# Summing the row partial sums of w_down by 32x32 VectorE transposes and selector matmuls, and merging two small copies at the start, in a decode kernel (conditioned layer norm, cached grouped attention, gated FFN)

## The chip, the cores and the metric

The kernel runs on one core of a Trainium2 chip. The metric is device time in microseconds (us) of one execution, as the median over several executions.

"The profile" below is the summary page of one profiled execution, with its views: groups, waits, chain of waits, timeline and windows. "The trace" is the record of every instruction and every DMA packet behind it. PE is TensorE's matmuls, PEld its weight loads, DVE VectorE, ACT ScalarE, POOL GpSimd, and SPq the SyncE queue that issues the loads.

## The reference, cut to what matters

```python
x = A_x                                        # 1 x 1 x 1024, bfloat16
mod = (_silu(c) @ w_mod).reshape(...)          # six modulation vectors of 1024
h = _layernorm(x) * (1 + ca) + sa
x = x + ga * attention(h, k_cache, v_cache, wq, wo)   # 32 heads, 4 kv heads, 65536 cached positions
h = _layernorm(x) * (1 + cb) + sb
x = x + gb * ((_gelu(h @ w_gate) * (h @ w_up)) @ w_down)  # F = 3584
```

Every weight and both caches are read once. There is one token, so the kernel moves 185.6 MB and computes little per byte.

## The kernel before

Loads are issued by SyncE into a ring of ten slots that are one tensor in SBUF, `slots`. SBUF tensors are placed one after the other in the order in which they are allocated.

```python
    ident = sb("ident", [P, P], dt.bfloat16)   # 256 bytes in each partition
    x_col = sb("x_col", [P, KD])               # 32 bytes
    x_nat = sb("x_nat", [P, KD])
    sg_col = sb("sg_col", [P, KD])
    th_col = sb("th_col", [P, KD])
    slot_all = nc.alloc_sbuf_tensor("slots", [P, NSLOT * SLOT], dt.bfloat16)
    identf = sb("identf", [P, P])
    ...
    c_col = sb("c_col", [P, KD])
```

The last product, with w_down, is done in two ways. Most of w_down ("early") is used as the moving operand, 512 columns at a time, against 32-column weights that hold the activations; the sums are rows, at partitions 0, 32, 64 and 96 of two PSUM banks. The part that lands last ("late": pieces of 1024, 512, 256 and 256 KB) is used as weights, 128x128 at a time, against one activation column, and accumulates columns in `acc_dn`. The rows must be added into those columns:

```python
        v = row_matvec(place_d, early, o_pad, (v_uc,), (NQ - 1, NROW * UE - NQ))
        v_rows = both(row_a, 2, P)             # PSUM -> SBUF: one half on VectorE, one on ScalarE
        late = j_d[len(early):]
        col_matvec(acc_dn, late[:1], o_pad[:, :, 0], KD, True)
        PE.wait(*v_rows)
        for j, a in enumerate(plain):          # 8 blocks of 128 columns, fp32
            pe.matmul(
                acc_dn[:, j:j + 1], row_a[:, a], ones1[:, :], start=False, stop=True, skip_group_check=True)
        v = col_matvec(acc_dn, late[1:], o_pad[:, :, 0], KD, False)
        # then: multiply by gb, add x1, one transpose, copy, store
```

Of the kernel before, what the change touches and what calls it, by code (L numbers as in the profile page):

```python
# [5 lines left out]
ACT = mybir.ActivationFunctionType  # L6
ALU = mybir.AluOpType
AX = mybir.AxisListType

P = 128  # L10
# [12 lines left out]
ROW = 512  # L23
QD = 32
# [56 lines left out]
def bass_adaLN_cond__gqa_block_cached__geglu_ffn__decode_kernel(  # L81
# [15 lines left out]
    KD = D // P  # L97
# [14 lines left out]
    scale = float(DH) ** -0.5  # L112
    NQ = P // QD
# [5 lines left out]
    PE = Eng(nc, nc.tensor, "c_pe")  # L119
    DVE = Eng(nc, nc.vector, "c_dve")  # L120
    AC = Eng(nc, nc.scalar, "c_act")
    GP = Eng(nc, nc.gpsimd, "c_pool")
    sp, pe, dve, act, pool = nc.sync, nc.tensor, nc.vector, nc.scalar, nc.gpsimd
# [4 lines left out]
    def sb(name, shape, d=dt.float32):  # L128
        return nc.alloc_sbuf_tensor(name, shape, d)

    ident = sb("ident", [P, P], dt.bfloat16)
    x_col = sb("x_col", [P, KD])
    x_nat = sb("x_nat", [P, KD])
    sg_col = sb("sg_col", [P, KD])
    th_col = sb("th_col", [P, KD])
    slot_all = nc.alloc_sbuf_tensor("slots", [P, NSLOT * SLOT], dt.bfloat16)
    identf = sb("identf", [P, P])
    ones1 = sb("ones1", [P, 1])
    onesf = ones1[:, :].to_broadcast([P, P])
    halfneg = sb("halfneg", [P, 1])  # L140
    c_col = sb("c_col", [P, KD])
    s_pad = sb("s_pad", [P, KD, QD], dt.bfloat16)
    h_pad = sb("h_pad", [P, KD, QD], dt.bfloat16)
    ga_nat = sb("ga_nat", [P, KD])
# [5 lines left out]
    x1_col = sb("x1_col", [P, KD])  # L150
# [10 lines left out]
    NR = P // REP  # L161
    m_sp = sb("m_sp", [P, 2, NR])
    rsel = sb("rsel", [P, NR])
    selt = sb("selt", [P, P])
    s_fp = s_pad[:, :, :].rearrange("p k c -> p (k c)").bitcast(dt.float32)
    mneg, al, zr = (s_fp[:, i * NC:(i + 1) * NC] for i in range(3))
# [8 lines left out]
    def ktf(half):  # L175
        return kt_sb[:, half, :, :].rearrange("p a b -> p (a b)").bitcast(dt.float32)
# [5 lines left out]
    row_a = ktf(1)[:, 0:2 * ROW]  # L182
# [10 lines left out]
    b6 = nc.alloc_psum_tensor("b6", [P, 512], dt.float32)  # L193
    b7 = nc.alloc_psum_tensor("b7", [P, 512], dt.float32)
    kt_fp = kt_ps[:, :].bitcast(dt.float32)
    tr_ps = sc_ps[:, 0:2 * ROW]
    acc_dn = b7[:, 64:64 + KD]
# [53 lines left out]
    def emit_all():  # L251
# [39 lines left out]
        for i in range(0, NC + KU, KU):  # L291
# [6 lines left out]
            if i >= KU:  # L298
                j = i - KU
# [53 lines left out]
        for a in [a for r in ev for a in r] + ex + m1 + oc + pc + kfill + vfill:  # L353
# [5 lines left out]
            selw[:, HQ - REP:HQ].unsqueeze(2), identf[:, :].rearrange("p (r h) -> p h r", h=REP), AX.X, ALU.add)  # L359
        dve.tensor_reduce(  # L360
            rsel[:, :].unsqueeze(2), identf[:, :].rearrange("p (r h) -> p r h", h=REP), AX.X, ALU.add)
        v = DVE.done(dve.tensor_reduce(
            dm4.unsqueeze(3), identf[:, :].rearrange("p (c b h) -> p c b h", c=NQ, h=REP), AX.X, ALU.add))
        DVE.wait(v)
# [3 lines left out]
        v_sel = DVE.done(dve.tensor_reduce(  # L368
            dmask[:, :].unsqueeze(2), dm4.rearrange("p c b -> p b c"), AX.X, ALU.add))
# [4 lines left out]
        PE.wait((x_sem, 16))  # L374
        v = PE.done(pe.matmul(b6[:, 2 * KD:3 * KD], x_row, ident[0:KD, 0:KD], start=True, stop=True))
        DVE.wait(v)
        cx = b6[:, 0:2 * KD].rearrange("p (k c) -> p c k", c=2)
        v_c = DVE.done(dve.tensor_copy(c_col[:, :], cx[:, 0, :]))
        AC.wait(v_c)
        v_th = AC.done(act.activation(th_col[:, :], c_col[:, :], ACT.Tanh, scale=0.5))  # L380
        dve.tensor_copy(x_col[:, :], cx[:, 1, :])
        v_x = DVE.done(dve.tensor_copy(x_nat[:, :], b6[:, 2 * KD:3 * KD]))
        DVE.wait(v_th)
        v = DVE.done(dve.tensor_scalar(sg_col[:, :], th_col[:, :], 0.5, 0.5, ALU.mult, ALU.add))
        DVE.wait(v)
        v_s = DVE.done(dve.tensor_tensor(s_pad[:, :, 0], c_col[:, :], sg_col[:, :], ALU.mult))

        def col_matvec(bank, jobs, rhs, nblk, first):

# [49 lines left out]
        def ln_norm(xin, ready, pscol):  # L439

            st = once("st", [P, 2])
            junk = once("junk", [P, KD])
            me = once("me", [P, 2])
            sq = once("sq", [P, 1])
            va = once("va", [P, 1])
            rs = once("rs", [P, 1])
            hn = once("hn", [P, KD])
            DVE.wait(ready)
            dve.reduce_sum(st[:, 0:1], xin, axis=AX.X)
            v = DVE.done(dve.tensor_tensor_reduce(junk[:, :], xin, xin, 1.0, 0.0, ALU.mult, ALU.add, st[:, 1:2]))  # L450
            PE.wait(v, t1)
            v = PE.done(pe.matmul(b6[:, pscol:pscol + 2], onesf, st[:, :], start=True, stop=True))
            DVE.wait(v)
            v = DVE.done(dve.tensor_scalar(me[:, :], b6[:, pscol:pscol + 2], 1.0 / D, None, ALU.mult))
            DVE.wait(v)
            v = DVE.done(dve.tensor_tensor(sq[:, :], me[:, 0:1], me[:, 0:1], ALU.mult))
            DVE.wait(v)
            v = DVE.done(
                dve.scalar_tensor_tensor(va[:, :], me[:, 1:2], LN_EPS, sq[:, :], ALU.add, ALU.subtract)  # L459
            )  # L460
            GP.wait(v, v_const)
            v = GP.done(pool.tensor_tensor(rs[:, :], va[:, :], halfneg[:, :], ALU.pow))  # L462
            DVE.wait(v)
            v = DVE.done(dve.tensor_scalar(hn[:, :], xin, me[:, 0:1], rs[:, 0:1], ALU.subtract, ALU.mult))
            return hn, v
# [18 lines left out]
        plain = [slice(j * P, (j + 1) * P) for j in range(KD)]  # L484
# [1 line left out]
        def quads(t, n, w=P):  # L486
            return t.rearrange("p (n g y) -> p n g y", n=n, g=w // QD)[:, :, :, 0]

        hn1, v_hn1 = ln_norm(x_col[:, :], v_x, 32)

        def place_m(k):
            for h in range(2):
# [38 lines left out]
        def place_2(b0, n):  # L531
# [5 lines left out]
        v = row_matvec(place_2(0, 2 * NQ), whole(j_q), h_pad, (v_h,), (0, KD - 1), rest_of_mod)  # L537
# [4 lines left out]
        v = turn(tr_ps, P, row_q, plain, P, (v_ra, v_rb))  # L542
        DVE.wait(v)
        v = DVE.done(dve.tensor_copy(
            q_col[:, :].rearrange("p (r g t) -> p r t g", r=2, g=NQ),
            quads(tr_ps, KD).rearrange("p (r t) g -> p r t g", r=2)))
# [146 lines left out]
        v_x = {}  # L693
# [96 lines left out]
        for g in range(Hkv):  # L790
            ins = pe.matmul(
                b6[0:HQ, 0:P + ZW], selw[:, HQ - REP * (g + 1):HQ - REP * (g + 1) + QD], o_red[:, g, :],
                start=g == 0, stop=g == Hkv - 1)
        v = PE.done(ins)
        DVE.wait(v)
        v = DVE.done(dve.reciprocal(rz[:, :], b6[0:HQ, P + ZW - 1:P + ZW]))
        DVE.wait(v)
        v = DVE.done(dve.tensor_scalar(oT[:, :], b6[0:HQ, 0:P], rz[:, 0:1], None, ALU.mult))
        PE.wait(v, v_const)
        w = P // QW  # L800
        for q in range(QW):
            ins = pe.matmul(
                b6[:, 352:352 + w], spread[:, QW - 1 - q:QW - 1 - q + P], oT[:, q * w:(q + 1) * w],
                start=q == 0, stop=q == QW - 1)
        v = PE.done(ins)
# [7 lines left out]
        def both(rows, b0, n):  # L813
            DVE.wait(v)
            x = DVE.done(dve.tensor_copy(rows[:, 0:ROW], kt_fp[:, b0 * ROW:(b0 + 1) * ROW]))  # L815
            AC.wait(v)
            y = AC.done(act.activation(  # L817
                rows[0:n, ROW:2 * ROW], kt_fp[0:n, (b0 + 1) * ROW:(b0 + 2) * ROW], ACT.Copy))
            return x, y

        last_ev = tuple(ev[(NC - 1) % SITES][b].tok(seen_by(NC - 1)) for b in range(NB))
        v = row_matvec(place_o, whole(j_o), o_pad, (v_opk,) + last_ev, (NQ - 1, HQ - NQ))
        t_att = sb("t_att", [P, KD])
        v_rows = both(row_a, 0, P)
        v = turn(tr_ps, P, row_a, mixed, P, v_rows)
# [2 lines left out]
        DVE.wait(v_ac)  # L828
        v = DVE.done(dve.tensor_tensor(t_att[:, :], t_att[:, :], mod_sb[:, 2, :], ALU.mult))
        DVE.wait(v)  # L830
        v_x1 = DVE.done(dve.tensor_tensor(x1_col[:, :], t_att[:, :], x_col[:, :], ALU.add))
        hn2, v = ln_norm(x1_col[:, :], v_x1, 34)
        v_tn = turn(tr_ps, P, row_a, plain, P, (v_ac,))
        v_h2 = modulate(h_pad, hn2, v, 3, 4)
# [1 line left out]
        v = DVE.done(dve.tensor_reduce(att_nat[:, :].unsqueeze(2), quads(tr_ps, KD), AX.X, ALU.add))  # L836
        DVE.wait(v)
        v_tf = v
        v = DVE.done(dve.tensor_tensor(att_nat[:, :], att_nat[:, :], ga_nat[:, :], ALU.mult))
# [19 lines left out]
        v = row_matvec(place_2(2, NBF), whole(j_g), h_pad, (v_h2,), (0, KD - 1))  # L859
        v_rows = both(row_g, 2, QD * (NBF - NQ))  # L860
        v_g = turn_f(row_g, v_rows + (v_tf,))
        DVE.wait(v_g)
        for dst, src in zip(parts(g1), parts_ps()):
            v = DVE.done(dve.tensor_copy(dst, src))
        v_g1 = v
        DVE.wait(v)
        v = DVE.done(dve.tensor_tensor(g2, g1, g1, ALU.mult))
        DVE.wait(v)
        v = DVE.done(dve.tensor_scalar(g3, g2, GELU_C, 1.0, ALU.mult, ALU.add))
        DVE.wait(v)  # L870
        v = DVE.done(dve.tensor_tensor(g4, g3, g1, ALU.mult))
        AC.wait(v)
        v = AC.done(act.activation(gth, g4, ACT.Tanh, scale=SQRT_2_OVER_PI))
        DVE.wait(v)
        v = DVE.done(dve.scalar_tensor_tensor(g2, gth, 1.0, g1, ALU.add, ALU.mult))
        v_g2 = v
        v = row_matvec(place_2(0, NBF), whole(j_u), h_pad, (v_h2,), (0, KD - 1))
        v_rows = both(row_u, 0, QD * (NBF - NQ))
# [7 lines left out]

        early = [a for a in j_d if a[2] < NROW * UE]
        v = row_matvec(place_d, early, o_pad, (v_uc,), (NQ - 1, NROW * UE - NQ))
        v_rows = both(row_a, 2, P)
        late = j_d[len(early):]  # L890
        col_matvec(acc_dn, late[:1], o_pad[:, :, 0], KD, True)
        PE.wait(*v_rows)
        for j, a in enumerate(plain):
            pe.matmul(  # L894
                acc_dn[:, j:j + 1], row_a[:, a], ones1[:, :], start=False, stop=True, skip_group_check=True)
        v = col_matvec(acc_dn, late[1:], o_pad[:, :, 0], KD, False)
        DVE.wait(v, v_xn)
        v = DVE.done(dve.tensor_tensor(t_dn, acc_dn, gb_nat[:, :], ALU.mult))
        DVE.wait(v)
        v = DVE.done(dve.tensor_tensor(y_col, t_dn, x1_nat[:, :], ALU.add))  # L900
        PE.wait(v)
        yT = b6[:, :].bitcast(dt.bfloat16)[0:KD, 768:768 + P]
        v = PE.done(pe.transpose(yT, y_col, ident[:, :]))
        DVE.wait(v)
        v = DVE.done(dve.tensor_copy(y_row, yT))
# [3 lines left out]
        assert issued[0] == len(loads)  # L909

    emit_all()
    return nc

# [27 lines left out]
```

## Time and profile before

| | before |
|---|---|
| median time | 439.82 us (3 runs, 438.96 to 439.94) |
| span of the profiled execution | 438.6 us |
| read from HBM | 185.60 MB, 423 GB/s over the span |
| last loads of w_down land at | 430.96, 432.21, 432.84, 433.49 us |

The landing times are the last of a load's 16 semaphore updates in the trace.

From the page of the kernel before: DMA is the busy share of the 16 DMA engines in 40 slices of the span, in tenths.

```profile
PE   0436559959696878959777895968779594675376
DMA  8999999999999999999999999999999999999994
GB/s 355 430 435 439 435 432 429 429 424 433 433 430 433 431 433 430 433 436 430 436 439 433 436 428 430 430 439 430 436 430 430 430 426 429 444 428 434 415 430 173
```

The DMA engines are full from the second slice to the last but one, so the kernel's time is the time of the loads plus what is left to do after the last of them.

The end of the timeline of the kernel before (start, duration of the merged group, engine, line, operation, out<-in, shapes, count, and the idle time before it with what ended it):

```profile
429.68 0.60 ACT L817 ACTIVATE kt_sb<-kt_ps 128x512 f32<-128x512 f32 x1 [9.14 <-PE kt_ps L419]
429.68 0.69 DVE L815 COPY kt_sb<-kt_ps 128x512 f32<-128x512 f32 x1 [6.82 <-PE kt_ps L419]
431.01 1.01 PE L396 MATMUL b<-p_row,slots 128*128 128x1 bf16 x32 [1.40 <-DMA slots<-in_B_w_down_dram]
431.89 3.55 PE L894 MATMUL b<-ones,kt_sb 128*128 128x1 f32 x16
435.30 0.99 PE L396 MATMUL b<-p_row,slots 128*128 128x1 bf16 x32
436.33 0.17 DVE L898 TENSOR_TENSOR kt_sb<-b,gb_nat 128x8 f32<-128x8 f32 x1 [5.96 <-PE b L396]
437.30 0.37 SPq L907 DMA_DIRECT2D out_dram<-kt_sb  x1
```

Line 894 is the eight fp32 matmuls that add the rows; each appears as two records. They occupy TensorE from 431.89 to 435.30 us, and the last 32 column matmuls (line 396) start behind them although their data had landed by 433.49 us. The chain of waits, which goes back from the last instruction to whatever released each step, runs through the block (start, duration, engine, tile, line, count; it counts the block from the end of the group ahead of it):

```profile
431.01 1.01 PE b L396 x32
432.02 3.41 PE b L894 x16
435.44 0.87 PE b L396 x32
```

### The profile page before, as it was taken

What the parts mean: (1) busy time and instruction counts of PE and PEld (TensorE: products, weight loads), DVE (VectorE), ACT (ScalarE), POOL (GpSimd) and SP (SyncE); (2) the same over time, 40 slices, a digit from 0 to 9 for tenths busy, and PEclk for the clock granted to TensorE, in tenths of its full rate; (3) what the DMA queues carried; (4) which work ended last, traced back from release to release, by engine and by line L of the source; (5) the groups of instructions that cost most, each with busy time, mean ns of one, the idle gap of its engine ahead of it and who ended that gap; (6) DMA issues with size and microseconds to landing.
All of it is one profiled execution on the core that took longest, in us unless ns stands there. A gap on an engine that the chain in (4) does not pass through costs nothing.

```text
span 438.6 us, 8499 instructions
## 1 busy us (share of the span) xinstructions
PE 305.5 (70%) x3892; PEld 203.4 (46%) x3892; DVE 206.9 (47%) x309; ACT 111.8 (25%) x165; POOL 16.8 (4%) x23
## 2 busy tenths in 40 slices
PE   0436559959696878959777895968779594675376
PEld 0112236636464556646555563646556362232124
DVE  6601025637383765827465673737477373421001
ACT  1000001533332523333351443324135334000000
POOL 9500000000000000000000000000000000000000
PEclk9995669999696988979897896969689798587665
DMA  8999999999999999999999999999999999999994
GB/s 355 430 435 439 435 432 429 429 424 433 433 430 433 431 433 430 433 436 430 436 439 433 436 428 430 430 439 430 436 430 430 430 426 429 444 428 434 415 430 173
DMA packets 7936, 185.77 MB, mean 424 GB/s; under 512 B 882, under 2 KB 882, under 8 KB 1268
## 3 DMA queue, kind: packets, MB, share of 16 engines
q1 hardware_dynamic: 7904, 185.60, 98.4%
q8 instruction: 8, 0.13, 0.1%
q14 instruction: 4, 0.03, 0.0%
q10 hardware_dynamic: 20, 0.01, 0.0%
HBM read 185.60 MB, written 0.00 MB: 423 GB/s over the span
## 4 chain that ended last, share of the span: by engine, by line
DMA 56%; PE 31%; DVE 10%; issue 1%; ACT 1%; POOL 0%; POOLq 0%; SPq 0%
DMA slots<-in_A_k_cache_dram 44%; PE kt_ps L597 16%; DMA slots<-in_B_w_down_dram 8%; PE b L667 4%; DMA slots<-in_A_v_cache_dram 4%; PE sc_ps L619 4%; PE kt_ps L419 3%; DVE selt L365 3%; DVE kt_sb L705 2%; DVE s_pad L739 1%; DVE o_red L728 1%; PE b L894 1%; PE sc_ps L648 1%; PE b L635 1%; DVE o_acc L716 1%
## 5 line engine op out<-in xcount | busy, mean ns | idle before, releaser
L597 PE MATMUL kt_ps<-ident,slots 128*128 128x128 bf16 x2048 | 156.8, 238 | 48.6 <-DMA slots<-in_A_k_cache_dram 47.9
L597 PEld LDWEIGHTS kt_ps<-ident,slots 128*128 128x128 bf16 x2048 | 136.1, 108 | 74.2 <-issue 41.8
L705 DVE COPY kt_sb<-kt_ps 128x2048 bf16<-128x2048 bf16 x96 | 117.5, 1224 | 111.5 <-PE kt_ps L597 109.8
L705 ACT ACTIVATE kt_sb<-kt_ps 128x2048 bf16<-128x2048 bf16 x32 | 60.1, 1877 | 27.7 <-PE kt_ps L597 27.7
L754 ACT ACTIVATE p_sb<-sc_ps 128x512 bf16<-128x512 bf16 x32 | 19.1, 597 | 182.4 <-PE sc_ps L648 182.4
L619 PE MATMUL sc_ps<-kt_sb,q_buf 128*32 128x512 bf16 x528 | 50.9, 420 | 0.0
L667 PE MATMUL b<-slots,p_sb 128*32 128x512 bf16 x560 | 40.1, 411 | 5.3 <-DMA slots<-in_A_v_cache_dram 4.6
L419 PE MATMUL kt_ps<-slots,h_pad 128*32 128x512 bf16 x176 | 18.0, 544 | 20.9 <-DMA slots<-in_B_w_up_dram 8.6
L716 DVE SCALAR_TENSOR_TENSOR o_acc<-o_acc,s_pad,b 128x512 f32<-128x512 f32 x28 | 20.9, 747 | 12.2 <-PE b L667 11.9
L635 PE MATMUL b<-m_sp,selt 128*128 128x16 f32 x66 | 13.0, 272 | 18.2 <-DVE m_sp L744 16.5
L667 PEld LDWEIGHTS b<-slots,p_sb 128*32 128x32 bf16 x560 | 15.5, 104 | 20.2 <-issue 5.2
L739 DVE TENSOR_REDUCE s_pad<-sc_ps 128x1 f32<-128x512 f32 x32 | 21.8, 680 | 0.0
L760 ACT ACTIVATE p_row<-sc_ps,s_pad 128x512 bf16<-128x512 f32 x32 | 21.6, 677 | 0.0
L635 PEld LDWEIGHTS b<-m_sp,selt 128*128 128x128 f32 x66 | 9.8, 188 | 23.7 <-DVE m_sp L744 21.4
L419 PEld LDWEIGHTS kt_ps<-slots,h_pad 128*32 128x32 bf16 x176 | 6.1, 125 | 30.8 <-issue 9.8
L815 DVE COPY kt_sb<-kt_ps 128x512 f32<-128x512 f32 x4 | 2.8, 692 | 33.5 <-PE kt_ps L419 33.5
L619 PEld LDWEIGHTS sc_ps<-kt_sb,q_buf 128*32 128x32 bf16 x528 | 10.9, 95 | 12.3 <-issue 4.5
L419 PE MATMUL kt_ps<-slots,s_pad 128*32 128x512 bf16 x96 | 10.9, 517 | 7.4 <-DMA slots<-in_w_mod_dram 7.4
L462 POOL TENSOR_TENSOR rs<-va,halfneg 128x1 f32<-128x1 f32 x2 | 1.1, 554 | 375.8 <-DVE va L459 375.8
L817 ACT ACTIVATE kt_sb<-kt_ps 128x512 f32<-128x512 f32 (+1 forms) x4 | 2.4, 595 | 49.0 <-PE kt_ps L419 49.0
L648 PEld LDWEIGHTS sc_ps<-ident,p_row 128*128 128x128 bf16 x136 | 7.8, 98 | 15.1 <-issue 14.4
L648 PE MATMUL sc_ps<-ident,p_row 128*128 128x128 bf16 x136 | 13.7, 224 | 0.2 <-ACT p_row L760 0.2
(107 smaller groups left out, 170.9 us busy)
## 6 DMA issues: line engine op xcount, KB each, us to landing
slots<-in_A_k_cache_dram SPq DMA_DIRECT2D x16, 4096.0 KB, 23.5
slots<-in_A_v_cache_dram SPq DMA_DIRECT2D x16, 4096.0 KB, 23.6
slots<-in_w_mod_dram SPq DMA_DIRECT2D x4, 3072.0 KB, 20.4
slots<-in_A_wq_dram SPq DMA_DIRECT2D x2, 4096.0 KB, 35.5
slots<-in_A_wo_dram SPq DMA_DIRECT2D x4, 2048.0 KB, 25.3
slots<-in_B_w_gate_dram SPq DMA_DIRECT2D x2, 3584.0 KB, 30.2
slots<-in_B_w_up_dram SPq DMA_DIRECT2D x2, 3584.0 KB, 29.5
slots<-in_B_w_down_dram SPq DMA_DIRECT2D x2, 2048.0 KB, 35.1
```

The costliest lines, as they stand in the source:

```text
L365: dve.tensor_scalar(selt[:, :].rearrange("p (r h) -> p r h", h=REP), selw[:, HQ - REP:HQ].unsqueeze(1).to_broadcast([P, NR, REP]), -scale, ...
L419: ins = pe.matmul(out, pad[:, k, :], view[:, kk, c0:c0 + ROW], start=k <= last_k[0], stop=k >= last_k[1], skip_group_check=True,)
L597: ins = pe.transpose(kt_ps[:, half * 2048 + t * P:half * 2048 + (t + 1) * P], j_k[i - i % KU].view[:, i % KU * CH + b * TB + t, :], ident[ ...
L619: ins = pe.matmul(sc(j)[QD * g:QD * (g + 1), :], q_buf[:, j % SITES, QD * b:QD * (b + 1)], kt_sb[:, j % 2, n:n + w, :].rearrange("p n d -> ...
L635: ins = pe.matmul(b6[:, 0:NR], selt[:, :], m_sp[:, j % 2, :], start=True, stop=True)
L648: ins = pe.transpose(sc_bf[:, o:o + P], p_row[:, j % 2, c * P:(c + 1) * P], ident[:, :])
L667: ins = pe.matmul(b7[QD * c:QD * (c + 1), :].rearrange("p (b d) -> p b d", b=NB), p_sb[:, s, c * P + QD * g:c * P + QD * (g + 1)], v[:, NQ ...
L705: ev[i % SITES][b].done(act.activation(dst, src, ACT.Copy) if E_ is AC else dve.tensor_copy(dst, src))
L716: v = oc[j % SITES].done(dve.scalar_tensor_tensor(o_acc[:, :], o_acc[:, :], al[:, j:j + 1], b7[:, :], ALU.mult, ALU.add))
L739: v = DVE.done(dve.tensor_reduce(m_new, sc(j), AX.X, ALU.max))
L754: pc[jt % SITES].done(act.activation(p_sb[:, jt % SITES, :], sc_bf[:, o:o + ROW], ACT.Copy))
L760: v_x[j] = ex[s].done(act.activation(p_row[:, j % 2, :], sc(j), ACT.Exp, bias=mneg[:, j:j + 1], scale=scale, accum_out=zr[:, j:j + 1],))
```

## The change

The intent is to shorten that fp32 block. The row sums are turned by two 32x32 block transposes on VectorE, straight out of PSUM; then four matmuls with a 32-column selector (each of its 32 columns picks the same partition out of every block of 32) add them into `acc_dn`, each into a quarter of its partitions. On the side, two copies at the start are merged into one, over a tile that holds both columns.

```diff
     ident = sb("ident", [P, P], dt.bfloat16)
-    x_col = sb("x_col", [P, KD])
+    cx_col = sb("cx_col", [P, 2, KD])
+    c_col, x_col = cx_col[:, 0, :], cx_col[:, 1, :]
     x_nat = sb("x_nat", [P, KD])
...
-    c_col = sb("c_col", [P, KD])
...
+    sel32 = sb("sel32", [P, QD])
...
+        dve.tensor_reduce(
+            sel32[:, :].unsqueeze(2), identf[:, :].rearrange("p (a r) -> p r a", r=QD), AX.X, ALU.add)
...
-        cx = b6[:, 0:2 * KD].rearrange("p (k c) -> p c k", c=2)
-        v_c = DVE.done(dve.tensor_copy(c_col[:, :], cx[:, 0, :]))
+        v_c = DVE.done(dve.tensor_copy(cx_col[:, :, :], b6[:, 0:2 * KD].rearrange("p (k c) -> p c k", c=2)))
...
-        dve.tensor_copy(x_col[:, :], cx[:, 1, :])
...
-        v_rows = both(row_a, 2, P)
+        DVE.wait(v)
+        for h in range(2):
+            v_rows = DVE.done(dve.transpose(
+                row_a[:, h * ROW:(h + 1) * ROW], kt_fp[:, (2 + h) * ROW:(3 + h) * ROW]))
         late = j_d[len(early):]
         col_matvec(acc_dn, late[:1], o_pad[:, :, 0], KD, True)
-        PE.wait(*v_rows)
-        for j, a in enumerate(plain):
+        PE.wait(v_rows, v_sel)
+        turned = row_a.rearrange("p (j a r) -> p a j r", a=NQ, r=QD)
+        for a in range(NQ):
             pe.matmul(
-                acc_dn[:, j:j + 1], row_a[:, a], ones1[:, :], start=False, stop=True, skip_group_check=True)
+                acc_dn[QD * a:QD * (a + 1), :], sel32[:, :], turned[:, a, :, 0],
+                start=False, stop=True, skip_group_check=True)
         v = col_matvec(acc_dn, late[1:], o_pad[:, :, 0], KD, False)
```

More of the change, by code (lines that the diff above doesn't have):

```diff
@@ L376, in emit_all @@
         DVE.wait(v)
-        cx = b6[:, 0:2 * KD].rearrange("p (k c) -> p c k", c=2)
-        v_c = DVE.done(dve.tensor_copy(c_col[:, :], cx[:, 0, :]))
+        v_c = DVE.done(dve.tensor_copy(cx_col[:, :, :], b6[:, 0:2 * KD].rearrange("p (k c) -> p c k", c=2)))
         AC.wait(v_c)
-        v_th = AC.done(act.activation(th_col[:, :], c_col[:, :], ACT.Tanh, scale=0.5))
-        dve.tensor_copy(x_col[:, :], cx[:, 1, :])
+        v_th = AC.done(act.activation(th_col[:, :], c_col, ACT.Tanh, scale=0.5))
         v_x = DVE.done(dve.tensor_copy(x_nat[:, :], b6[:, 2 * KD:3 * KD]))
@@ L385, in emit_all @@
         DVE.wait(v)
-        v_s = DVE.done(dve.tensor_tensor(s_pad[:, :, 0], c_col[:, :], sg_col[:, :], ALU.mult))
+        v_s = DVE.done(dve.tensor_tensor(s_pad[:, :, 0], c_col, sg_col[:, :], ALU.mult))
         def col_matvec(bank, jobs, rhs, nblk, first):
@@ L487, in quads @@
             return t.rearrange("p (n g y) -> p n g y", n=n, g=w // QD)[:, :, :, 0]
-        hn1, v_hn1 = ln_norm(x_col[:, :], v_x, 32)
+        hn1, v_hn1 = ln_norm(x_col, v_x, 32)
         def place_m(k):
@@ L830, in emit_all @@
         DVE.wait(v)
-        v_x1 = DVE.done(dve.tensor_tensor(x1_col[:, :], t_att[:, :], x_col[:, :], ALU.add))
+        v_x1 = DVE.done(dve.tensor_tensor(x1_col[:, :], t_att[:, :], x_col, ALU.add))
         hn2, v = ln_norm(x1_col[:, :], v_x1, 34)
```

## The prediction

> **What bounds the kernel now.** The loads. The page gives 185.6 MB at 424 GB/s and a DMA share of 9 tenths or more in nearly every slice; the windows view shows 389 to 434 GB/s right up to 431 us. The last three pieces of w_down land (last of 16 semaphore updates) at 432.21, 432.84 and 433.49 us. Only work after the last landing is exposed. The timeline shows that tail:
>
> - 429.68: accumulated row sums leave PSUM, one 128x512 half on VectorE (0.69 us), the other at the same time on ScalarE (0.60 us)
> - 431.01: the first late piece lands; its 32 column matmuls have a pitch of 27 ns (to 431.86)
> - 431.86 to 435.30: eight fp32 matmuls against ones, each with 128 columns of weights and one of data; they appear as 16 records at a pitch of 213 ns, 3.41 us
> - 435.30 to 436.29: the last 32 column matmuls, whose data had all landed by 433.49
> - then multiply, add, transpose, copy and the store, to 438.6
>
> So the last piece waits in SBUF for 2.4 us, until 435.92, because of the fp32 block.
>
> **What the change does.** Removed: the 16 records (3.41 us), the ScalarE eviction. Added: two VectorE 32x32 block transposes of 128x512 fp32 out of PSUM, one after the other; four fp32 matmuls with 32 columns of weights and 8 of data; one small reduction and one copy fewer at the start.
>
> Transposes: "VectorE: DVE Perf Modes", section "The three transpose paths", gives 311 ns for 128x128 bf16; the VectorE copy of the same 128x512 fp32 shape takes 0.69 us here. Estimate from these: 0.7 us each, so the rows are ready near 431.15, still before TensorE finishes the first late piece at 431.86. Hidden, with 0.7 us to spare.
>
> Selector matmuls: eight records. A quarter of the weight columns suggests a quarter of 213 ns, about 55 ns each; "TensorEngine Tiling (Array Packing)", section "Key Properties", says tiles can work in parallel but that a change of mode drains. Estimate 0.4 to 0.8 us with a drain on both sides, over near 432.5.
>
> The rest then follows the landings: 16 matmuls from 432.5 to 432.95, 8 to 433.2, and the last 8 wait for 433.49 plus about 0.05, ending near 433.9 instead of 436.29. Gain 2.4 us; part of what is removed disappears in the new wait for the last load, which also absorbs 0.35 us more in the selector matmuls.
>
> The head does not count: VectorE's operations up to 16.5 us wait while POOL fills buffers, and the queue holds loads well past that moment (DMA share about 1 through that time).
>
> **Prediction.** 439.8 - 2.4 = 437.4 us, range 436.4 to 438.5. Faster by over 2%: 0.01; within 2%: 0.97; slower by over 2%: 0.02.
>
> **What the profile would show if right.** The loads and everything to 429.7 us unchanged; eight selector records taking under 0.8 us; a short TensorE idle time before the last 8 column matmuls, released by the w_down DMA; the chain of waits going from the w_down DMA directly to the last column matmuls; the span about 2.4 us shorter.
>
> **What would make it wrong.** Transposes of fp32 out of PSUM at half rate or worse (over 1.3 us each would delay TensorE); selector matmuls that don't overlap or drains costing over a microsecond (the gain falls toward 1.5 us); a different landing time of the last load, which shifts the end one for one; loads disturbed by the changed start.

## More of the kernel before

The windows view of the kernel before, in three stretches (start:end, length, busy time and count of each engine, then granted TensorE clock, DMA share, GB/s):

```profile
160.00:200.00 40.00, 31.05 (x415) 22.04 (x414) 23.65 (x33) 13.41 (x20) 0.00 (x0) 0.87 1.01 434
200.00:240.00 40.00, 31.90 (x441) 22.85 (x439) 23.73 (x35) 13.39 (x20) 0.00 (x0) 0.87 1.00 433
240.00:280.00 40.00, 31.05 (x431) 22.07 (x429) 24.37 (x35) 14.90 (x22) 0.00 (x0) 0.87 1.00 434
```

## The result, and the profile after

The changed kernel took 439.88 us (median of 6, 439.72 to 440.15); the kernel before took 439.75 us in the same comparison. The ratio is 1.0006, with a 95% interval of 0.9993 to 1.0019. A ratio here is the mean time of one kernel's fast runs over that of the other's from the same rounds, so it is not quite the ratio of the medians. There was no gain, and the range of the prediction missed.

The end of the timeline after:

```profile
431.93 1.31 DVE L892 STREAM_TRANSPOSE kt_sb<-kt_ps 128x512 f32<-128x512 f32 x2 [7.00 <-PE kt_ps L420]
433.32 1.01 PE L397 MATMUL b<-p_row,slots 128*128 128x1 bf16 x32 [1.47 <-DMA slots<-in_B_w_down_dram]
434.27 0.29 PE L899 MATMUL b<-kt_sb,sel 128*32 128x8 f32 x8
434.58 1.03 PE L397 MATMUL b<-p_row,slots 128*128 128x1 bf16 x24
435.89 0.37 PE L397 MATMUL b<-p_row,slots 128*128 128x1 bf16 x8 [0.28 <-DMA slots<-in_B_w_down_dram]
436.30 0.17 DVE L904 TENSOR_TENSOR kt_sb<-b,gb_nat 128x8 f32<-128x8 f32 x1 [3.06 <-PE b L397]
437.27 0.37 SPq L913 DMA_DIRECT2D out_dram<-kt_sb  x1
```

The tail itself does what was expected. The fp32 block went from 3.55 us to 0.29 us (line 899), the transposes took 1.31 us and were done before TensorE needed them, and TensorE now idles for 0.28 us until the last load lands. But the final multiply on VectorE starts at 436.30 us, against 436.33 before.

The difference is in where the tail starts: the first late piece was used at 433.32 us instead of 431.01. The chain of waits after ends in the load:

```profile
408.93 26.92 DMA slots<-in_B_w_down_dram
435.85 0.05 issue
435.89 0.38 PE b L397 x8
```

The last load landed at 435.85 us; before, at 433.49. The loads got 2.36 us slower, and the tail 2.4 us faster. Where was that time lost? The same three stretches of the windows view, after:

```profile
160.00:200.00 40.00, 31.30 (x439) 21.71 (x432) 25.07 (x34) 13.43 (x20) 0.00 (x0) 0.87 1.00 431
200.00:240.00 40.00, 30.89 (x415) 22.11 (x413) 22.07 (x32) 13.13 (x19) 0.00 (x0) 0.83 1.00 432
240.00:280.00 40.00, 31.64 (x439) 22.39 (x437) 24.88 (x35) 13.91 (x21) 0.00 (x0) 0.87 1.01 432
```

The DMA share is still 1, but at 431 or 432 GB/s instead of 433 or 434. No wait was added; the loads are slower while they run. The landing times from the trace show a steady drift, not a step:

| load | before, us | after, us | later by |
|---|---|---|---|
| last of w_mod | 32.70 | 32.64 | -0.06 |
| second of wq | 52.88 | 53.05 | 0.16 |
| a K load | 154.79 | 155.63 | 0.84 |
| a K load | 251.60 | 252.85 | 1.25 |
| last V load | 372.63 | 374.42 | 1.79 |
| last of w_down | 433.49 | 435.85 | 2.36 |

The durations of single DMA packets in the trace show it at its root (percentiles, ns):

```
packet      kernel    5%    50%   95%    mean     count
32768 B     before   1213  1213  1213   1213.76   4352
32768 B     after    1214  1216  1224   1218.67   4352
 4096 B     before    159   159   159    159.0     128
 4096 B     after     159   161   167    161.7     128
24576 B     before    912   912   933    933.1     512
24576 B     after     912   912   933    932.8     512
```

Before, nearly every packet of a size takes exactly the same time. After, the 32 KB packets are 1 to 11 ns longer. Only the first loads, w_mod (24576 B packets), are nearly untouched: their median is 912 ns in both, and only for those that start after 30 us did it move, to 915 ns. Over all packets the durations add up to 6918 us before and 6950 us after; the difference, over 16 engines, is 2.0 us of the 2.36.

### The profile page after: what moved, and what is told of

It reads as the page before. It is cut to its first block, busy times and chain, and to the rows that moved or that the text cites. A ratio compares the mean times of both kernels' runs of the same rounds, so it can differ in the third digit from the quotient of the medians.

```text
span 438.5 us, 8482 instructions
## 1 busy us (share of the span) xinstructions
PE 307.3 (70%) x3884; PEld 202.2 (46%) x3884; DVE 207.6 (47%) x310; ACT 111.3 (25%) x164; POOL 16.8 (4%) x23
## 4 chain that ended last, share of the span: by engine, by line
DMA 58%; PE 29%; DVE 10%; SPq 1%; issue 1%; ACT 0%; POOL 0%; POOLq 0%
DMA slots<-in_A_k_cache_dram 44%; PE kt_ps L598 16%; DMA slots<-in_B_w_gate_dram 8%; DMA slots<-in_B_w_down_dram 6%; PE sc_ps L620 5%; PE b L668 4%; DVE selt L368 3%; DVE kt_sb L706 3%; PE kt_ps L420 2%; DVE s_pad L740 1%; PE b L636 1%; SPq L239 1%; DVE o_red L729 1%; PE sc_ps L649 1%; DVE o_acc L717 1%
## 5 line engine op out<-in xcount | busy, mean ns | idle before, releaser
L706 DVE COPY kt_sb<-kt_ps 128x2048 bf16<-128x2048 bf16 x96 | 117.6, 1225 | 110.9 <-PE kt_ps L598 109.2
L420 PE MATMUL kt_ps<-slots,h_pad 128*32 128x512 bf16 x176 | 19.3, 578 | 20.3 <-DMA slots<-in_B_w_up_dram 9.9
L420 PE MATMUL kt_ps<-slots,s_pad 128*32 128x512 bf16 x96 | 11.8, 549 | 6.5 <-DMA slots<-in_w_mod_dram 6.5
L750 DVE TENSOR_REDUCE s_pad<-b 128x1 f32<-128x16 f32 x32 | 5.6, 175 | 14.6 <-PE b L636 14.6
```

The costliest lines, as they stand in the source:

```text
L420: ins = pe.matmul(out, pad[:, k, :], view[:, kk, c0:c0 + ROW], start=k <= last_k[0], stop=k >= last_k[1], skip_group_check=True,)
L706: ev[i % SITES][b].done(act.activation(dst, src, ACT.Copy) if E_ is AC else dve.tensor_copy(dst, src))
```

## Experiments

The new tail comes 400 us after the drift starts, so it seemed an unlikely cause. What else differs is where things lie. The built program lists the address of each tile: `slots` starts at byte 16896 of each partition in the kernel before, which is 66 x 256, and at 16928 in the changed one, because `cx_col` ahead of it is 32 bytes larger than the `x_col` that it replaced. The Trainium skill, page "DMA: Bandwidth & Descriptors", section "How a descriptor splits into AXI transactions", says that a descriptor is split into transactions of 256 bytes, and that one that does not start on a multiple of 256 costs extra beats of the bus. It says so of reads; here the HBM side is as before and the side that is written moved.

Theory A: the shift of the slots slows the loads. Rival B: the new tail does, whatever the addresses. Rival C: it belongs to the run or to where the inputs lie in HBM. Four kernels were run together on one chip, five rounds each; the kernel before took 439.80 us there.

### 1. The new tail alone

```diff
# against the changed kernel
-    cx_col = sb("cx_col", [P, 2, KD])
-    c_col, x_col = cx_col[:, 0, :], cx_col[:, 1, :]
+    x_col_t = sb("x_col", [P, KD])        # and c_col behind the slots, as before;
+    x_col = x_col_t[:, :]                 # two separate copies at the start, as before
```

> Only the transposes and selector matmuls of the change; the two small copies stay separate, so the load slots start at SBUF byte 16896 again, as in the kernel before (the full change starts them at 16928). Theory A (the 32-byte shift of the slots makes every load packet 3 to 11 ns longer): 32 KB packets back at 1213 ns, last landing near 433.5 us, time 437.4 us. Theory B (the new tail itself slows the loads, whatever the addresses): packets up to 1224 ns, time 439.9. Theory C (the slower loads belong to the run or to where the inputs lie in HBM, not to the program's addresses): no relation to the edit, anything between 437.4 and 439.9, or differing between executions.

Measured: 437.59 us (437.44 to 437.76), ratio 0.9953 (0.9940 to 0.9967). 32 KB packets took 1213 ns at the 5%, 50% and 95% points, and the last load landed at 433.39 us. Rival B falls: the new tail is in this kernel and the loads are at full speed.

### 2. The kernel before, with nothing but an allocation moved

```diff
# against the kernel before
     th_col = sb("th_col", [P, KD])
+    c_col = sb("c_col", [P, KD])
     slot_all = nc.alloc_sbuf_tensor("slots", [P, NSLOT * SLOT], dt.bfloat16)
...
-    c_col = sb("c_col", [P, KD])
```

> The kernel before with one 32-byte tile (c_col) allocated ahead of the slots instead of behind them; no instruction changes, the slots start at 16928. Theory A: last landing near 435.85 us as with the full change, and the old tail follows 2.8 us after it, so 439.8 + 2.4 = 442.2 us. Theories B and C: 439.8, packets at 1213 ns.

Measured: 442.10 us (440.98 to 442.19), ratio 1.0056 (1.0042 to 1.0070). The 32 KB packets have the same durations as in the changed kernel (1214, 1216, 1224 ns; mean 1218.67), and the last load landed at 435.66 us. No instruction was added, removed or reordered, so rivals B and C fall both: this move of 32 bytes costs 2.3 us.

Two things moved along with what the loads write. TensorE reads the slots at the shifted addresses too, and three small tiles behind the slots (`identf`, `ones1`, `halfneg`), which no load writes, are shifted with them in every slow kernel. The traces show that neither is needed for the delay. In the changed kernel 172 of the 32 KB packets that started after 35 us ran while no engine executed an instruction, and they too took 1214, 1216 and 1224 ns at the three percentiles; 191 such packets in the kernel before took 1213 ns at all three.

The same stretches of the windows view as above, in this kernel, are slower in two of three; the first has 433 GB/s, within 1 GB/s of the kernel before. A stretch of 40 us is too coarse for a difference of 0.4%, and the packets and landings carry the argument:

```profile
160.00:200.00 40.00, 30.73 (x416) 21.70 (x408) 23.87 (x33) 13.42 (x20) 0.00 (x0) 0.87 1.01 433
200.00:240.00 40.00, 32.81 (x443) 22.93 (x436) 23.44 (x35) 13.12 (x19) 0.00 (x0) 0.87 1.00 431
240.00:280.00 40.00, 30.91 (x411) 21.61 (x410) 23.24 (x31) 13.42 (x20) 0.00 (x0) 0.87 1.00 430
```

### 3. The whole change, with the slots back in place

```diff
# against the changed kernel
-    cx_col = sb("cx_col", [P, 2, KD])
-    c_col, x_col = cx_col[:, 0, :], cx_col[:, 1, :]
+    sb("pad", [P, KD])                    # 32 bytes
...
     halfneg = sb("halfneg", [P, 1])
+    cx_col = sb("cx_col", [P, 2, KD])     # behind the slots
+    c_col, x_col = cx_col[:, 0, :], cx_col[:, 1, :]
```

> The full change, with the merged tile moved behind the slots and a 32-byte pad in its place, so that the slots start at 16896 again; same instructions as the full change. Theory A: 437.4 us. Theory B: 439.9. Theory C: no relation to the edit.

Measured: 437.57 us (437.37 to 437.60), ratio 0.9951 (0.9938 to 0.9965). This is the version that beats both kernels. The rate in the windows view is back:

```profile
160.00:200.00 40.00, 31.35 (x441) 21.93 (x434) 25.00 (x35) 13.41 (x20) 0.00 (x0) 0.87 1.00 433
200.00:240.00 40.00, 31.06 (x417) 22.21 (x414) 22.37 (x34) 13.12 (x19) 0.00 (x0) 0.83 1.00 433
240.00:280.00 40.00, 31.43 (x431) 22.50 (x429) 24.62 (x34) 14.78 (x22) 0.00 (x0) 0.87 1.01 435
```

The end of its timeline:

```profile
429.71 1.31 DVE L893 STREAM_TRANSPOSE kt_sb<-kt_ps 128x512 f32<-128x512 f32 x2 [6.81 <-PE kt_ps L421]
431.04 1.01 PE L398 MATMUL b<-p_row,slots 128*128 128x1 bf16 x32 [1.40 <-DMA slots<-in_B_w_down_dram]
431.99 0.29 PE L900 MATMUL b<-kt_sb,sel 128*32 128x8 f32 x8
432.34 1.00 PE L398 MATMUL b<-p_row,slots 128*128 128x1 bf16 x24
433.57 0.38 PE L398 MATMUL b<-p_row,slots 128*128 128x1 bf16 x8 [0.23 <-DMA slots<-in_B_w_down_dram]
433.98 0.17 DVE L905 TENSOR_TENSOR kt_sb<-b,gb_nat 128x8 f32<-128x8 f32 x1 [2.96 <-PE b L398]
434.95 0.37 SPq L914 DMA_DIRECT2D out_dram<-kt_sb  x1
```

The final multiply starts at 433.98 us, 2.35 us earlier than before, with the same landings as before. It still waits for the last load, which landed at 433.52 us.

### 4. The merged copy alone, with the old tail

The edit is the diff of the change without its last block, and without `sel32`; the slots start at 16928.

> Only the merged copy at the start, as the change has it, with the old tail; the slots start at 16928. Theory A: 442.2 us, the same as the kernel before with the slots shifted, since the merged copy itself is worth nothing. Theories B and C: 439.8.

Measured: 442.46 us (441.56 to 442.54), ratio 1.0065 (1.0051 to 1.0078); last landing at 435.80 us. The side edit, done by itself, makes the kernel 2.7 us slower, and experiments 1 and 3 (437.59 us without the merged copy, 437.57 with it) show that what the merged copy does is worth nothing either way: it is its tile's place that costs. Experiment 4 is 0.36 us slower than experiment 2, which was not followed up. (Their last landings are 0.14 us apart, but the two profiled runs, 440.98 and 441.56 us, are each the fastest of their five.)

### 5 to 7. Which start addresses are fast

These are all the realigned change of experiment 3 with the slots moved; they and experiment 8 ran together on another chip, five rounds each, with the kernel before at 439.84 us.

```diff
# e5: slots at 16960          # e6: slots at 17024          # e7: slots at 16640
-    sb("pad", [P, KD])       -    sb("pad", [P, KD])       (ident allocated behind
+    sb("pad", [P, 24])       +    sb("pad", [P, 40])        the slots, not ahead)
```

> The realigned change with a larger pad: slots at 16960, 64 bytes past a multiple of 256. Theory A1 (what counts is a start on a multiple of 256 bytes[...]): packets longer than 1213 ns, 439.9 us, as with a shift of 32. Theory A2 (a start on a multiple of 64 bytes is enough): 437.5 us and 1213 ns.

> The realigned change with slots at 17024, 128 bytes past a multiple of 256. A1 (256 counts): 439.9 us and longer packets. A2, or 128 being enough: 437.5 us and 1213 ns.

> The realigned change with the identity tile moved behind the slots: slots at 16640, a multiple of 256 but not of 512. A1: 437.5 us, packets at 1213 ns. If a multiple of 512 were needed: 439.9 us.

| start of the slots | modulo 256 | kernel | median us | 32 KB packet, 5/50/95%, ns | last landing, us |
|---|---|---|---|---|---|
| 16896 | 0 | e3 | 437.57 | 1213 / 1213 / 1213 | 433.52 |
| 16640 | 0 | e7 | 437.56 | 1213 / 1213 / 1213 | 433.50 |
| 16928 | 32 | the change | 439.88 | 1214 / 1216 / 1224 | 435.85 |
| 16960 | 64 | e5 | 439.48 | 1213 / 1215 / 1222 | 435.43 |
| 17024 | 128 | e6 | 439.34 | 1213 / 1215 / 1225 | 435.69 |

Packets and landings are those of the profiled run; that of e6 was the slowest of its five, with 439.75 us. The rows of e3 and of the change come from other comparisons, in which the kernel before took 439.80 and 439.75 us.

A start on a multiple of 256 bytes is fast, whether or not it is one of 512 (16640 is not); starts 32, 64 and 128 bytes past one are slow, nearly alike. A start on a multiple of 64 or 128 is not enough. So A1 holds as to where the loads are fast. The guess of 439.9 us was 0.4 to 0.6 us too high at 64 and 128: the penalty there is somewhat smaller than at 32.

### 8. The realigned change without the selector matmuls

```diff
-        for a in range(NQ):
-            pe.matmul(
-                acc_dn[QD * a:QD * (a + 1), :], sel32[:, :], turned[:, a, :, 0],
-                start=False, stop=True, skip_group_check=True)
```

> The realigned change without the four selector matmuls (the result is wrong on purpose: the row sums are left out). If the tail is now set by the last landing, as in the realigned run, where TensorE waits about 0.3 us for it: same time, 437.5 us. If the selector matmuls and their drains are still exposed: about 0.3 us less, 437.2.

The result is wrong on purpose (relative error 0.108). Measured: 437.58 us (437.54 to 437.61), against 437.56 with them in experiment 7, which ran beside it. The selector matmuls are now free: the tail begins at the last landing, and nothing that is done ahead of it on TensorE can gain more.

## Why the prediction was wrong

- *"So the last piece waits in SBUF for 2.4 us [...] because of the fp32 block"*: right. With the loads as before, removing the block gave 2.35 us in the timeline and 2.2 us in the medians (439.80 to 437.57).
- *Transposes 0.7 us each, hidden*: right; 1.31 us for the two, 0.67 and 0.72 each. They ended at 431.02 us in experiment 3, before the selector matmuls at 431.99. What proved a good guide is the 0.69 us of the VectorE copy of the same shape. The Trainium skill's 311 ns ("VectorE: DVE Perf Modes", "The three transpose paths") is for a 128x128 bfloat16 block, a quarter of the elements; no run here times that one.
- *Selector matmuls 0.4 to 0.8 us with drains*: at most the lower end, 0.29 us for the eight records and 0.35 us from the first of them to the next matmul in experiment 3. Within each half of the eight, the records of the four quarters start 7 ns apart, where the column matmuls with 128 columns of weights start 27 ns apart. This agrees with "TensorEngine Tiling (Array Packing)", "Key Properties", that tiles run in parallel. The cost of a drain at the change of mode isn't shown: the first selector record starts 95 ns after the matmul ahead of it, and the next matmul starts 0.05 us after its own piece landed (432.29 us), so that it may have waited for that alone.
- *The rest follows the landings, a new wait for the last load*: right, 0.23 us of idle time in experiment 3, and experiment 8 shows that nothing else is exposed.
- ***"The loads and everything to 429.7 us unchanged"*: this is the step that failed.** The last landing moved from 433.49 to 435.85 us. The prediction named such a shift as what could make it wrong, but saw no reason for it. It read the diff as instructions ("one copy fewer at the start") and not as a layout: a tile ahead of the load slots grew by 32 bytes. Every load into the slots then began off a multiple of 256 bytes, and nearly every packet after the first 32 us became longer (1218.7 ns on average instead of 1213.8 for 32 KB). The 2.36 us lost there happen to equal the 2.4 us gained in the tail. That the two cancel is an accident: experiments 1 and 2 have each without the other, at 437.59 and 442.10 us around 439.80.

What is not settled is how a shift becomes 1 to 11 ns. Counting beats does not give it: by the account in the section on AXI transactions named above, an offset of 32 bytes would waste one beat of 32 bytes and an offset of 128 four (an estimate from its rule), yet 32 was the slowest of the three. Nor is the shift enough by itself: the w_mod loads, to equally shifted addresses, took 912 ns at the median in every kernel. Of the 32 KB packets that started between 30 and 35 us, 92% in experiment 5 and 98% in experiment 6 still had their 1213 ns, against 6% in the changed kernel.

The delay isn't confined to packets that write the slots, either. The profile lists fetches of instructions as queues of their own. The 16 KB packet that queue 8 moves near 84 us took 954 ns in all five kernels with the slots on a multiple of 256 bytes, and 1094 or 1095 ns in all five with the slots off one. So the shifted loads also hold up other traffic, by 140 ns here against the 1 to 11 ns of a 32 KB load packet; transfers that get in each other's way would look like this, but where they meet no run here shows.

## What to carry to other kernels

When a kernel is bound by its loads, allocate the tensors that the loads write so that they start on a multiple of 256 bytes (16640 and 16896 were fast here; 32, 64 and 128 bytes past one were slow), say so in the source, and check the address after every edit that adds or resizes a tile ahead of them; here 32 bytes cost half a per cent, as much as a 3.4 us block of matmuls was worth. When a change that shortens the tail gives nothing, compare the landing times of the loads before looking at the tail. Test the parts of a change apart: one of them may be undoing the other.

## What the Trainium skill lacked or had wrong

- "DMA: Bandwidth & Descriptors", "How a descriptor splits into AXI transactions", speaks of an unaligned start for reads. The runs show that the start of the *written* side in SBUF counts too: 32 KB packets 1213 ns at a multiple of 256 bytes, 1214 to 1224 ns (5% to 95%) at 32 past it; 439.80 us became 442.10 us by a move of 32 bytes alone. Instruction fetches slowed as well: 954 ns became 1094 or 1095 for the one near 84 us.
- The same section's count of wasted beats does not rank the offsets: mean of a 32 KB packet 1213.8 ns at 0, 1218.7 at 32, 1217.7 at 64, 1217.5 at 128 bytes. The first loads (24576 B packets) were hardly slowed, with 912 ns at the median in every kernel.
- "SBUF — State Buffer", "Operand start alignment", gives the element size as the rule and says that it is about legality, not speed. No page gives the rule for speed that the runs show: 256 bytes for the destination of loads, with 64 and 128 not enough (439.48 and 439.34 us against 437.57).
- "TensorE: Matmul & The Clock Gate", section "Part 1: The HAM clock gate", says that the number of matmuls at the slow clock varies from run to run; it has no case like this one, of a block near the end that nothing hides. In the profiled run of experiment 2 the old fp32 block took 2.63 us instead of 3.55, with a mean granted clock over the block of 0.71 instead of 0.50 in the kernel before (its records started 112 ns apart at first and then 213, instead of 213 throughout), and that run took 440.98 us against 442.09 to 442.19 for the other four. Experiment 4 repeats it: 2.71 us at 0.68, and 441.56 us against 442.42 to 442.54. The kernel before has such a run too (438.81 among eight of 439.67 to 439.83), though that one has no profile, so that its cause is the same is only likely.
